# A long-convolution block with an MLP on one Trainium2 core: taps' spectra loaded back in quarters, residuals and joins given to TensorE, and a new order of the operations

## The chip, the cores and the metric

The kernel runs on one core of a Trainium2 chip. Its time is the device time of one execution in microseconds (us); lower is better. A core has a matrix engine (TensorE, PE in the profile), a vector engine (VectorE, DVE), a scalar engine (ScalarE, ACT), a general engine (GpSimd, POOL) and a queue engine (SyncE, SP) that issues most transfers. Each engine works through its own instructions in the order in which they were written and waits for the others through semaphores.

## The reference

All inputs are bfloat16: u is 2048 rows by 512 channels, the state-space part has 128 states for each channel, and the MLP is 512 to 1376 to 512.

```python
def _A_ref(u, A_re, A_im, B_re, B_im, C_re, C_im, log_dt, Dskip):
    ...
    P = jnp.exp(logdA[:, :, None] * l[None, None, :])         # 512 x 128 x 2048, complex
    K = jnp.einsum("dn,dnl,dn->dl", Cc, P, dB).real           # the taps: 512 x 2048
    ...
    Yf = Uf * Kf[None, :, :, :]                               # the spectra of u and of the taps, padded to 4096
    y = irfft2(Yf)[:, :, 0, :L] ...
    return y + u * Dskip[None, None, :]

x = A_u
h = x + _A_ref(_layernorm(x, axis=-1), ...)
h2 = h + (gelu(_layernorm(h) @ w1 + b1) @ w2 + b2)            # tanh form of gelu
```

The layer norm runs over the 512 channels of a row.

## The kernel before, in words

**Tiling.** The 2048 rows are cut into two blocks b = 0 and 1 of 1024, and each block into two halves sb of 512. The 512 channels are cut into four chunks c of 128. The taps are handled for two chunks at a time: q = 0 holds chunks 0 and 1, q = 1 holds chunks 2 and 3. The output of block 1 needs two products of spectra (its own input with the near taps, and block 0's with the far taps), that of block 0 needs one.

**Stages, in the order in which most of the work comes.**

1. Tables: ACT computes exponentials and sines (L1068 is the last kind) from arguments that TensorE writes to PSUM (L1059). DVE multiplies them (L1030, then L1072 for chunks 2 and 3). In the same time the rows of u are normalized: `stats` takes the power on POOL (L926), `unorm` applies it (L947 on DVE or L949 on ACT).
2. Taps: `kgen` (L1101, L1102) makes the taps of chunks 0 and 1 from these products, `kgen4` (L1132, L1133) those of chunks 2 and 3; the result is copied out of PSUM, and a small DVE addition of Dskip (L1115, L1142) ends a chunk.
3. Spectra of the taps, for each q: `carry` issues four small DMAs (L1152) that put a copied strip behind the taps; `kspec` (L1167) transforms in two parts, of which the second needs the carry; `kstage` writes its result to DRAM in two DMAs of 512 KB (the tensor AK_d) and loads it back with another arrangement in two DMAs of 512 KB; `fstage` (L981) works on four of the sixteen f at a time. `lstage` (L1195, L1214) makes the far taps' spectra by way of small DMAs on POOL's queue (AL_d).
4. Spectra of u: `xspec` (L961, L981), block 0 and then block 1.
5. `inverse(b, c, ...)`: for each half fh DVE makes the product (L1243; for block 1 two products and a sum, L1248), for block 1 two more DVE additions join the four parts to two (L1251), and TensorE transforms back: 16 matmuls of 64x128 for two terms, 32 for four (L1259). The result is copied out and transposed by a DMA (L1265).
6. `tail(b, sb)`: TensorE's last step of the transform (L1329); the residual h = u + y, by an identity matmul on TensorE for b = 0, sb = 0 (L1324, then a copy out of PSUM) and by a DVE addition elsewhere (L1336); statistics of the second layer norm (L1339 and small operations); its application (L1352 on DVE or L1354 on ACT); and a transpose.
7. `mlp(b, sb)`: w1 (L1383), gelu on ACT (L1385), w2 (L1405), the residual on DVE (L1407), and the output's DMAs.

**PSUM and copies.** PSUM is used as four slots of 128x1024 float32 (ps_64 to ps_67 in the listings below). Copies out of PSUM have the lines L542 (ACT) and L544 (DVE), whoever asked for them.

**What sets the order.** Each call adds operations to a list. The table ORDER is a permutation of the list's numbers, and the instructions are written in that order; a negative number stands for the second of two engines on which an operation may run. A planner (`Sched.run`) walks through ORDER with costs in us. Its costs don't change the order: they choose which PSUM slot an operation gets, and where the planner sees TensorE idle for over 0.4 us it writes filling matmuls (L1510, an identity matmul of 128x512 whose result nobody reads). Each POOL computation is made to wait for the last DVE instruction written ahead of it.

## Time and profile before

| | before |
|---|---|
| time, median of 3 runs | 236.28 us (236.27 to 236.67) |
| the profiled execution | 235.89 us, of which 234.0 us are the span in the trace |
| TensorE busy | 200.7 us (86%), 2809 matmuls |
| ScalarE busy | 177.3 us (76%) |
| VectorE busy | 170.0 us (73%) |
| GpSimd busy | 39.8 us (17%) |
| mean granted TensorE clock | 0.997 |

The share of an engine is an average over stages with different limits, so it has to be read by stretches of the span. Rows with "x" give a number of instructions; "ar" is SBUF, "ps" is PSUM; the arrow points from the input to the output. "PEld" is TensorE's loading of weights, which runs beside its matmuls. A row of the chain of waits tells what the last-ending work was waiting for at that time: start, duration, engine, output, line. A "[... <-X]" behind a row is the idle time ahead of it and what ended it.

### The profile page before, as it was taken

What the parts mean: (1) busy time and instruction counts of PE and PEld (TensorE: products, weight loads), DVE (VectorE), ACT (ScalarE), POOL (GpSimd) and SP (SyncE); (2) the same over time, 40 slices, a digit from 0 to 9 for tenths busy, and PEclk for the clock granted to TensorE, in tenths of its full rate; (3) what the DMA queues carried; (4) which work ended last, traced back from release to release, by engine and by line L of the source; (5) the groups of instructions that cost most, each with busy time, mean ns of one, the idle gap of its engine ahead of it and who ended that gap; (6) DMA issues with size and microseconds to landing.
All of it is one profiled execution on the core that took longest, in us unless ns stands there. A gap on an engine that the chain in (4) does not pass through costs nothing.

```text
span 234.0 us, 6711 instructions
## 1 busy us (share of the span) xinstructions
PE 200.7 (86%) x2809; PEld 106.9 (46%) x2809; DVE 170.0 (73%) x304; ACT 177.3 (76%) x217; POOL 39.8 (17%) x185
## 2 busy tenths in 40 slices
PE   4206898868888899999989988899999999999993
PEld 2102633325666685456753343344444444444552
DVE  4969989998997764798999889889934884022021
ACT  5999999999999898999989897787275106806600
POOL 7950760000055520040000110100000101000000
PEclk9999999999999999999999999999999999999998
DMA  5692220100000163875589922235632072053103
GB/s 170 165 197 55 59 36 11 37 1 3 3 6 6 30 146 68 244 202 183 112 140 198 311 96 41 49 66 104 114 66 38 0 139 66 0 111 79 34 20 72
DMA packets 39246, 20.33 MB, mean 87 GB/s; under 512 B 26738, under 2 KB 37012, under 8 KB 39216
## 3 DMA queue, kind: packets, MB, share of 16 engines
q1 hardware_dynamic: 38510, 19.28, 36.1%
q0 software_dynamic: 256, 0.30, 0.8%
q8 instruction: 22, 0.36, 0.6%
q10 hardware_dynamic: 450, 0.33, 0.5%
q14 instruction: 8, 0.07, 0.1%
HBM read 8.10 MB, written 4.49 MB: 54 GB/s over the span
## 4 chain that ended last, share of the span: by engine, by line
PE 41%; ACT 13%; DVE 7%; DMA 5%; issue 4%; POOL 3%; SPq 1%; ACTq 0%; DVEq 0%
PE ps L1405 16%; PE ps L1383 13%; ACT ar L542 9%; DMA ar<-ar 3%; PE ps L1329 2%; ACT ar L1068 2%; DMA ar<-AK_d 2%; PE ps L1259 2%; PE ps L981 2%; ACT ar L1385 2%; DVE ar L1248 2%; DVE ar L1243 1%; POOL ar L926 1%; PE ps L961 1%; POOL ar L1466 1%
## 5 line engine op out<-in xcount | busy, mean ns | idle before, releaser
L542 ACT CAST ar<-ps 128x1024 bf16<-128x1024 f32 (+3 forms) x75 | 66.6, 965 | 11.8 <-PE ps L1259 5.1
L1385 ACT ACTIVATE ar<-ps,ar 128x512 bf16<-128x512 f32 (+1 forms) x44 | 28.6, 687 | 25.0 <-PE ps L1383 24.5
L1383 PE MATMUL ps<-ar 128*128 128x512 bf16 (+1 forms) x176 | 40.4, 379 | 1.5 <-ACT ar L542 1.1
L1405 PE MATMUL ps<-ar 128*128 128x512 bf16 (+3 forms) x187 | 39.6, 367 | 0.0
L1068 ACT ACTIVATE ar<-ps 128x1024 bf16<-128x1024 int16 x36 | 34.5, 1058 | 0.5 <-PE ps L1059 0.5
L1407 DVE TENSOR_TENSOR ar<-ps,ar 128x512 bf16<-128x512 f32 (+1 forms) x17 | 10.8, 653 | 29.5 <-PE ps L1405 16.3
L1243 DVE TENSOR_TENSOR ar<-ar 128x2048 bf16<-128x2048 bf16 x24 | 28.8, 1220 | 3.8 <-PE ps L1259 3.0
L1405 PEld LDWEIGHTS <-ar 128*128 128x128 bf16 (+1 forms) x187 | 18.0, 98 | 19.9 <-issue 0.4
L1383 PEld LDWEIGHTS <-ar 128*128 128x128 bf16 (+1 forms) x176 | 17.1, 100 | 21.7 <-issue 3.0
L1059 PE MATMUL ps<-ar 128*32 128x512 f16 (+1 forms) x368 | 21.6, 331 | 5.7 <-ACT ar L1068 5.6
L544 DVE CAST ar<-ps 128x1024 bf16<-128x1024 f32 (+3 forms) x20 | 21.2, 1075 | 7.0 <-PE ps L1133 3.0
L1510 PE MATMUL ps<-ar 128*128 128x512 bf16 x53 | 14.6, 412 | 13.6 <-DMA ar<-in_A_u_dram 12.2
L1030 DVE TENSOR_TENSOR ar<-ar 128x2048 bf16<-128x2048 bf16 x21 | 24.8, 1214 | 0.8 <-ACT ar L1068 0.4
L926 POOL TENSOR_TENSOR ar<-ar 128x4 f32<-128x4 f32 (+1 forms) x6 | 9.3, 1544 | 93.9 <-DVE ar L603 42.2
L801 ACT ACTIVATE ar<-ar 128x1024 bf16<-128x1024 f32 x16 | 15.7, 1041 | 1.1 <-DVE ar L613 1.1
L1059 PEld LDWEIGHTS <-ar 128*32 128x32 f16 x368 | 9.3, 97 | 15.8 <-issue 13.5
L961 PE MATMUL ps<-ar 128*32 128x512 bf16 x256 | 15.9, 380 | 0.2 <-ACT ar L542 0.2
L1259 PE MATMUL ps<-ar 64*128 64x128 bf16 x384 | 13.6, 217 | 1.1 <-ACT ar L542 1.1
L1510 PEld LDWEIGHTS <-ar 128*128 128x128 bf16 x53 | 4.9, 102 | 21.0 <-issue 17.5
L1259 PEld LDWEIGHTS <-ar 64*128 64x128 bf16 x384 | 11.1, 94 | 6.7 <-issue 2.7
L619 DVE SCALAR_TENSOR_TENSOR ar<-ar 128x4 f32<-128x4 f32 (+5 forms) x37 | 10.2, 282 | 5.3 <-POOL ar L926 3.5
L981 PE MATMUL ps<-ar 128*32 128x512 bf16 (+1 forms) x256 | 13.0, 328 | 0.2
(118 smaller groups left out, 293.7 us busy)
## 6 DMA issues: line engine op xcount, KB each, us to landing
ar<-in_A_u_dram SPq DMA_DIRECT2D x4, 512.0 KB
AK_d<-ar SPq DMA_DIRECT2D x4, 512.0 KB
ar<-AK_d SPq DMA_DIRECT2D x4, 512.0 KB
out_dram<-ar SPq DMA_DIRECT2D x30, 64.0 KB
ar<-in_B_w_dram SPq DMA_DIRECT2D x4, 344.0 KB
ar<-ar SPq DMA_DIRECT2D x20, 64.0 KB
ar<-in_B_w_dram SPq DMA_DIRECT2D x2, 640.0 KB
AL_d<-ar POOLq DMA_DIRECT2D x8, 36.0 KB, 4.0
```

The lines of the kernel that those rows point to most:

```text
L542: act.copy(out_fn(), in_fn())
L544: dve.tensor_copy(out_fn(), in_fn())
L961: pe.matmul(pst(p)[32 * cg:32 * cg + 32, 512 * z:512 * z + 512], lhsT=BD.ap()[:, 32 * f + 2 - 2 * jl:32 * f + 34 - 2 * jl], rhs=un[2 * (2 ...
L1030: dve.tensor_tensor(o, o[:, 1].unsqueeze(1).to_broadcast([P] + list(o.shape[1:])), f[:, :, ::-1, ::-1] if rev else f, ALU.mult)
L1059: pe.matmul(pst(p)[32 * g:32 * g + 32, 256 * j:256 * (j + n)].rearrange("p (a b) -> p a b", a=n), lhsT=W2[DELTAS.index(d)].ap(), rhs=S2[g] ...
L1068: add("ACT", c_act(1024), lambda e, o_=o_, i_=i_: act.activation(o_(), i_(), ACT.Sin, scale=SINSC), r=[p, TBL], w=[sc[cs]])
L1243: dve.tensor_tensor(pieces(o).rearrange("p z (a r d) -> p a z r d", a=4, r=2), k, x, ALU.mult)
L1259: pe.matmul(pst(p)[:, 512 * h + 128 * k:512 * h + 128 * k + 128], lhsT=o[z].ap()[rows, k, r, :], rhs=TP[w].ap()[rows, f0 // 2 + k, :], sta ...
L1383: pe.matmul(pst(p)[:fs, 512 * z:512 * z + 512], lhsT=w1s[dc].ap()[:, fc * P:fc * P + fs], rhs=ybuf.ap().rearrange("p (t c) k -> p c t k", ...
L1385: add("ACT", c_act(512, 1), lambda e, p=p, z=z, fc=fc, fs=fs: act.activation(hT.ap()[:fs, fc, :], pst(p)[:fs, 512 * z:512 * z + 512], ACT. ...
L1405: pe.matmul(pst(p)[:, 512 * z + c0:512 * z + c1], lhsT=hT.ap()[:fs, fc, 128 * t:128 * t + 128], rhs=w2s[fc].ap()[:fs, c0:c1], start=(fc == ...
L1510: pe.matmul(slots[z][:, 0:512], lhsT=identb.ap(), rhs=hs[15].ap(), start=True, stop=True)
```

## The change

It has four parts.

- `kstage` loads AK_d back in four DMAs of 256 KB for each q, where there were two of 512 KB; each quarter is one group of `fstage`.
- `tail(0, 1)` puts the residual on TensorE by identity matmuls, as `tail(0, 0)` did: four matmuls of 128x512 more, four DVE additions fewer, and four copies of 128x512 out of PSUM in their place (three on ACT, one on DVE).
- `inverse(1, c)` for c = 0 and 1 leaves out the two DVE joins of each half (8 of 16 in all) and lets TensorE work on four terms: 64 more matmuls of 64x128.
- ORDER is another permutation; the planner's costs for POOL's power (0.3 to 1.5), `kgen4` (0.13 to 0.146) and `tail` (0.85 throughout) are others.

```diff
@@ ORDER
-    49, 1, 0, 50, 2, 12, 15, 5, 52, 11, 13, 40, 3, 16, 88, 74, 17, 167, 4, 51, 43, 18, 19, 73, ...
+    1, 49, 12, 15, 0, 50, 88, 2, 16, 146, 14, 4, 17, 3, 166, 13, 18, 11, 19, 52, 89, 20, 21, 51, ...
@@ stats
-        POOL(0.3, lambda: gp.tensor_tensor(buf[3].ap(), buf[1].ap(), mhalf.ap().to_broadcast([P, n]), ALU.pow), ...
+        POOL(1.5, lambda: gp.tensor_tensor(buf[3].ap(), buf[1].ap(), mhalf.ap().to_broadcast([P, n]), ALU.pow), ...
@@ kgen4
-                add("PE", 0.13 * h, fn, r=[EA2, Br, IA2, Bi], w=[p], new=[p] if b == 0 else [], hv=1)
+                add("PE", 0.146 * h, fn, r=[EA2, Br, IA2, Bi], w=[p], new=[p] if b == 0 else [], hv=1)
@@ kstage
-        for fh in range(2):
-            dma("SP", lambda fh=fh: kf[8 * fh:8 * fh + 8].ap(), lambda fh=fh: D.rearrange("s (q f) d -> (s q) f d", f=16)[:, 8 * fh:8 * fh + 8, :], 524288, [("AK", q, 0), ("AK", q, 1)], [kf[8 * fh:8 * fh + 8], ("KFR", q, fh)], k=0.7)
+        for f0 in range(0, 16, 4):
+            dma("SP", lambda f0=f0: kf[f0:f0 + 4].ap(), lambda f0=f0: D.rearrange("s (q f) d -> (s q) f d", f=16)[:, f0:f0 + 4, :], 262144, [("AK", q, 0), ("AK", q, 1)], [kf[f0:f0 + 4]], k=0.7)
@@ inverse
-            if b:
+            mix = b and c > 1
+            if mix:
                 for r, op in enumerate((ALU.subtract, ALU.add)):
...
-            terms = [(0, 0, 0), (0, 1, 2)] if b else [(0, 0, 0), (1, 1, 1), (0, 1, 2), (1, 0, 2)]
+            terms = [(0, 0, 0), (0, 1, 2)] if mix else [(0, 0, 0), (1, 1, 1), (0, 1, 2), (1, 0, 2)]
...
-            add("PE", 0.235 * len(terms), fn, r=(o[:1] if b else o) + TP, w=[p], new=[p])
+            add("PE", 0.235 * len(terms), fn, r=(o[:1] if mix else o) + TP, w=[p], new=[p])
@@ tail
-                    if first:
+                    if b == 0:
                         pe.matmul(o, lhsT=identb.ap(), rhs=hs[8 * b + j].ap(), start=True, stop=False)
...
-            add("PE", 0.85 if first else 0.43 * (1 + b), fn, ...
+            add("PE", 0.85, fn, ...
...
-                if not first:
+                if b:
                     add("DVE", c_dve(512, 1, True), lambda e, src=src, hh=hh: dve.tensor_tensor(hh.ap(), src(), hh.ap(), ALU.add), ...
```

Over the whole program this makes 960 operations of 964, and 47 filling matmuls of 53 (from the spectra on 17 of 22). Of the copies out of PSUM and the second layer norm, some change engine: four copies of `kspec` go from ACT to DVE, four of 128x4x256 from DVE to ACT, and four applications L1354 from ACT to DVE as L1352. One line is added ahead of `inverse`'s end, so lines from L1249 on are one higher after the change (L1251 becomes L1252, L1329 becomes L1330).

**VectorE where the taps of chunks 0 and 1 end.** The rows are VectorE's, before, from the first product of chunks 2 and 3 that stands ahead of chunk 0's addition; `128x33x10` is a copy of taps of chunk 1, the small L619 and L603 belong to the layer norm of u, and the L619 behind L1115 uses the power that POOL computes.

```order
L1072 TENSOR_TENSOR ar<-ar 128x16x128 x2
L1115 TENSOR_TENSOR ar<-ar 128x32
L619 SCALAR_TENSOR_TENSOR ar<-ar 128x8
L1072 TENSOR_TENSOR ar<-ar 128x16x128
L947 TENSOR_SCALAR ar<-ar 128x512
L603 TENSOR_TENSOR ar<-ar 128x8
L1072 TENSOR_TENSOR ar<-ar 128x16x128
L544 CAST ar<-ps_67 128x33x10
L1115 TENSOR_TENSOR ar<-ar 128x32
```

The same place after the change:

```order
L1072 TENSOR_TENSOR ar<-ar 128x16x128
L1115 TENSOR_TENSOR ar<-ar 128x32
L934 BN_STATS ar<-ar 128x6
L544 CAST ar<-ps_64 128x33x10
L1115 TENSOR_TENSOR ar<-ar 128x32
L1072 TENSOR_TENSOR ar<-ar 128x16x128
L619 SCALAR_TENSOR_TENSOR ar<-ar 128x8
L1072 TENSOR_TENSOR ar<-ar 128x16x128 x2
L619 SCALAR_TENSOR_TENSOR ar<-ar 128x8
```

The second L1115, which completes the taps of q = 0, stood behind four products L1072 and behind the L619 that waits for POOL; now it stands behind one product and ahead of that L619. On TensorE the two parts of `kspec` for q = 0, with `lstage`'s L1195 between them, now follow one another ahead of all of `kgen4`; before, 48 matmuls of `kgen4` stood ahead of the second part. They stand behind the last L1059, as before. The four matmuls L1451 (a selection of table rows that L1214 needs), which stood between the last L1059 and `kspec`, now stand amid block 0's inverse.

**SP's queue of transfers around the spectra.** Before, from the carry of q = 0 on (`ar<-ar 7x...` is a carry, AK_d_68 is q = 0, AK_d_69 is q = 1, in_B_w_dram are weights of the MLP):

```order
L1152 DMA ar<-ar 7x2048 x4
L554 DMA AK_d_68<-ar 128x8x256 x2
L1152 DMA ar<-ar 7x32x64 x4
L554 DMA ar<-AK_d_68 128x2048 x2
L554 DMA AK_d_69<-ar 128x8x256 x2
L554 DMA ar<-in_B_w_dram 96x512
L554 DMA ar<-AL_d_70 18x4x256 x4
L554 DMA ar<-AK_d_69 128x2048 x2
```

And after:

```order
L1152 DMA ar<-ar 7x2048 x4
L554 DMA AK_d_68<-ar 128x8x256 x2
L554 DMA ar<-AK_d_68 128x1024 x3
L554 DMA ar<-in_B_w_dram 128x5x512
L1152 DMA ar<-ar 7x32x64 x3
L554 DMA ar<-in_B_w_dram 128x1376
L1152 DMA ar<-ar 7x32x64
L554 DMA ar<-AK_d_68 128x1024
L554 DMA ar<-in_B_w_dram 128x1376
L554 DMA ar<-AL_d_70 18x4x256
L554 DMA AK_d_69<-ar 128x8x256 x2
```

Three quarters of q = 0 now stand ahead of the carry of q = 1, and weights of 640 KB (128x5x512) and twice 344 KB (128x1376) stand between the quarters, the carry and the rest; before, these weights came after the first transposes.

**VectorE in the stretch where block 0's tail meets block 1's inverse.** Before, from the pair of products behind the statistics of block 0's first half:

```order
L1243 TENSOR_TENSOR ar<-ar 128x4x2x256 x2
L1352 TENSOR_SCALAR ar<-ar 128x512
L1248 TENSOR_TENSOR ar<-ar 128x2048
L1336 TENSOR_TENSOR ar<-ps_64,ar 128x512
L1251 TENSOR_TENSOR ar<-ar 128x4x128
L1339 BN_STATS ar<-ar 128x6
L1251 TENSOR_TENSOR ar<-ar 128x4x128
L1336 TENSOR_TENSOR ar<-ps_64,ar 128x512
L1339 BN_STATS ar<-ar 128x6
L1243 TENSOR_TENSOR ar<-ar 128x4x2x256
```

And after:

```order
L1243 TENSOR_TENSOR ar<-ar 128x4x2x256
L1340 BN_STATS ar<-ar 128x6
L619 SCALAR_TENSOR_TENSOR ar<-ar 128x4
L1353 TENSOR_SCALAR ar<-ar 128x512 x3
L1243 TENSOR_TENSOR ar<-ar 128x4x2x256
L1340 BN_STATS ar<-ar 128x6
L1248 TENSOR_TENSOR ar<-ar 128x2048
L1340 BN_STATS ar<-ar 128x6
L1243 TENSOR_TENSOR ar<-ar 128x4x2x256 x2
L1340 BN_STATS ar<-ar 128x6
```

The residual additions (L1336) and the joins (L1251) are gone from here; three applications of the second layer norm (L1353) stand together where one stood.

6 lines of the change are left out of this document (3 added, 3 removed), and 66 rows, old and new, of the table ORDER.

## The prediction

> **What bounds the kernel now.** I read the busy time of each engine by stretches first, then the chain of waits, then single groups. Columns of the stretches: length, TensorE (PE) with its matmuls, weight loads, DVE, ACT, POOL, granted clock, DMA share, GB/s.
>
> ```profile
> 5.00:77.00 72.00, 50.22 (x1135) 29.12 (x1139) 66.25 (x134) 71.15 (x84) 24.95 (x112) 1.00 0.23 50
> 70.00:77.00 7.00, 5.50 (x219) 4.11 (x211) 5.42 (x12) 7.00 (x10) 3.29 (x1) 1.00 0.02 5
> 77.00:98.40 21.40, 21.33 (x360) 13.76 (x360) 14.40 (x28) 19.13 (x24) 4.23 (x5) 1.00 0.47 116
> 98.40:118.00 19.60, 19.21 (x496) 12.79 (x497) 17.45 (x17) 18.55 (x21) 2.40 (x4) 1.00 0.69 178
> 118.00:136.00 18.00, 16.98 (x246) 7.72 (x246) 15.35 (x24) 16.70 (x20) 1.55 (x2) 1.00 0.90 225
> 136.00:154.00 18.00, 15.27 (x145) 7.22 (x144) 16.36 (x26) 15.41 (x22) 1.06 (x1) 1.00 0.17 34
> 154.00:224.00 70.00, 69.84 (x392) 32.26 (x391) 35.52 (x65) 33.81 (x50) 2.02 (x2) 1.00 0.35 68
> ```
>
> Until 77 us the tables bound it: ACT is busy for 71.15 of 72 us. From 77 on TensorE does. Its idle time is 0.07 + 0.39 up to 118, 1.02 + 2.73 from 118 to 154, and 0.16 behind: 4.2 us up to 154, of which 3.75 lie in the two stretches from 118. In those DVE is busy for 15.35 and 16.36 of 18, and the chain runs over it:
>
> ```profile
> 134.99 0.57 PE ps L1259 x16
> 135.59 2.36 DVE ar L1243 x2
> ...
> 145.41 1.01 ACT ar L542
> ```
>
> So three things change the end: when TensorE's closed stretch starts (about 77), what work it holds, and the holes from 118 to 154.
>
> **The change part by part.** The sum is made on the profiled execution: span 234.0, time 235.89, so 1.89 around it. The median 236.28 is 0.39 above, which I add at the end.
>
> *Start of the closed stretch.* The rows at its edge:
>
> ```profile
> 74.47 2.00 ACT L1068 ACTIVATE ar<-ps 128x1024 bf16<-128x1024 int16 x2
> 76.29 0.88 ACT L949 ACTIVATE ar<-ar 128x512 bf16<-128x512 bf16 x1
> 74.55 0.64 PE L1059 MATMUL ps<-ar 128*32 128x256 f16 x16
> 75.00 0.40 PE L1451 MATMUL ps<-ar 128*32 128x512 bf16 x4
> 76.92 1.04 PE L1167 MATMUL ps<-ar 20*128 20x512 bf16 x16 [0.94 <-DVE ar L1115]
> 71.65 0.20 DVE L1115 TENSOR_TENSOR ar<-ar 128x32 bf16<-128x32 bf16 x1
> 73.32 0.17 DVE L619 SCALAR_TENSOR_TENSOR ar<-ar 128x8 f32<-128x8 f32 x1 [1.48 <-POOL ar L926]
> 76.69 0.18 DVE L1115 TENSOR_TENSOR ar<-ar 128x32 bf16<-128x32 bf16 x1
> 77.61 1.16 DVE L1072 TENSOR_TENSOR ar<-ar 128x2048 bf16<-128x2048 bf16 x1
> ```
>
> The first part of `kspec` waits for the L1115 at 76.69, which stands in DVE's queue behind the 1.48 us wait for POOL and several products. With L1115 ahead of those, what holds `kspec` is the last L1059 group in front of it. That needs a slot which the third last sine frees: the sines end at 74.47 + 2.00 = 76.47, two sines of 1.0 earlier is 74.47, and with 0.64 of matmuls it is 75.1. So the stretch starts 76.92 − 75.1 = **1.8 us** earlier. The bounds are 0.8 (the last L1059 held by one sine more) and 2.4 (it ends at 74.55, when it began here). The four L1451 leave this gap and come back inside the closed stretch: **+0.4**.
>
> The second part of `kspec` now follows without the `kgen4` that covered the carry. SP's queue prices that:
>
> ```profile
> 76.92 3.04 SPq L1152 DMA_DIRECT2D ar<-ar  x4
> 82.28 1.04 PE L1167 MATMUL ps<-ar 27*128 27x512 bf16 x16
> ```
>
> Issuing the carry takes 3.04 us from the last L1115 on. Landing took at most 82.28 − 79.96 = 2.3 us more, since nothing waited for it. That L1115 comes at about 72 in the new order: the 71.65 at which the first one starts here, less one product of 1.16, plus a copy and a BN_STATS of about 1.1 and the table work before. The carry is then down by 72 + 5.3 = 77.3. The second part is due at 75.1 + 1.04 + 1.1 (L1195, the same size by columns) = 77.2. I take nothing; at worst 0.3 us, and the copies of `kgen4` that wait in turn would be late by as much.
>
> *Work added to TensorE.* A set of 16 matmuls L1259 costs 0.57 us (chain row above) and one of 32 costs 1.08; the residual is read from the tail of block 0, both forms of which the chain shows:
>
> ```profile
> 120.46 1.08 PE ps L1259 x32
> 127.80 0.55 PE ps L1329 x4
> 128.35 0.32 PE ps L1324
> 128.68 0.34 PE ps L1329 x2
> 132.83 1.62 PE ps L1510 x7
> ```
>
> Joins: four groups of 16 become 32, 4 × (1.08 − 0.57) = +2.04. Residual: a quarter of a tail costs 0.55 / 2 = 0.275 without the identity matmul and 0.32 + 0.34 = 0.66 with it, 4 × 0.385 = +1.54. Together **+3.6 us**. All of it lies in the closed stretch or in front of it, so it counts whole unless it falls into a hole.
>
> *Filling matmuls.* From the spectra on there are 17 instead of 22, at 1.62 / 7 = 0.23 us each: 5 × 0.23 = **−1.2**. A filling matmul costs time only where work stood ready behind it; at worst they go and leave idle time, 0.
>
> *The holes.* The groups in 118 to 154, by form (busy us, mean ns):
>
> ```profile
> L1251 DVE TENSOR_TENSOR ar<-ar 128x512 bf16<-128x512 bf16 x8 | 3.3, 419 | 0.0
> L1336 DVE TENSOR_TENSOR ar<-ps,ar 128x512 bf16<-128x512 f32 x4 | 2.6, 682 | 0.0
> L542 ACT CAST ar<-ps 128x512 bf16<-128x512 f32 x4 | 2.1, 588 | 0.6 <-PE ps L1329 0.6
> L1510 PE MATMUL ps<-ar 128*128 128x512 bf16 x22 | 5.4, 380 | 0.9 <-ACT ar L542 0.9
> L1354 ACT ACTIVATE ar<-ar 128x512 bf16<-128x512 bf16 x3 | 2.2, 806 | 0.0
> L1352 DVE TENSOR_SCALAR ar<-ar 128x512 bf16<-128x512 bf16 x1 | 0.4, 409 | 0.0
> ```
>
> DVE loses 3.3 (joins) and 2.6 (additions) and gains one copy of about 0.65 and two or three L1352 (0.4 each, 1.0): −4.3 of its 31.7 us here. ACT gains three copies, 3 × 0.59 = 1.8, and loses two or three L1354 at 0.81, about 2: no change. The idle 3.75 us and the 5.4 us of filling both come from waits for DVE's products and for what DVE hands to ACT. DVE's queue gets 4.3 us shorter, and the matmuls added (3.6) want room just there. I let TensorE's 4.2 us of idle time shrink by **−3.0**. The bounds: 0, if ACT, unchanged and at 32.1 of 36 us, sets the pace instead; −4.2, if every hole closes. I am nearer to the second because the relief of DVE is larger than all the holes, and DVE, not ACT, carries most pieces of the chain from 135.59 to 145.4.
>
> *The quarters.* In the chain the load of AK_d ends at 93.38 + 4.98 = 98.4, but next to nothing stood idle for it:
>
> ```profile
> 93.38 4.98 DMA ar<-AK_d
> 93.38 1.01 SPq L554 DMA_DIRECT2D ar<-AK_d  x2
> 89.91 3.35 SPq L1152 DMA_DIRECT2D ar<-ar  x4
> ```
>
> The work in between is `xspec`'s, which is ready beforehand; the stretch 77 to 98.4 has 0.07 us idle. Issuing two loads takes 1.01 us of SP's time, so two more cost SP 1.0 per q, hidden as long as the `xspec` work lasts. They now stand ahead of the carry of q = 1, and so are issued earlier than at 93.38. I take 0. The bounds: −0.13 (a third of the 0.39 idle in the next stretch) and +3 (rivals 2 and 5).
>
> **The sum.** −1.8 + 0.4 + 3.6 − 1.2 − 3.0 = −2.0. The profiled execution would come to 233.9, and with 0.39 the forecast is **234.3 us**.
>
> **The rivals.**
>
> 1. *ACT takes DVE's place, slower.* The place is 118 to 154, where ACT is busy for 32.1 of 36 us and is handed three copies. If the holes stay because copies out of PSUM arrive no earlier, the added 3.6 count whole: −1.8 + 0.4 + 3.6 − 1.2 = +1.0, **237.3 us**. It decides once less than 1 us of idle time is taken up. For it: the largest releasers of the groups there are copies L542 (0.9 before L1510). Against it: the chain from 135.59 to 145.4 is DVE but for single pieces. Chance 0.20.
> 2. *Weights ahead of the carry, no change.* In the new queue 640 KB and 344 KB of weights stand ahead of the last carry of q = 1 and of the fourth quarter. At the 317 GB/s that the best stretch shows, they take 3.1 us:
>
> ```profile
> 130.00:136.00 6.00, 6.00 (x71) 2.45 (x72) 4.37 (x13) 5.56 (x8) 1.55 (x2) 1.00 0.98 317
> ```
>
>    A carry that lands that late holds the second part of `kspec` for q = 1 and with it half of the spectra. About 1 us lies under `xspec`, so TensorE stands for 2 us: 234.3 + 2 = **236.3 us**. Against it: the DMA share from 77 to 98.4 is 0.47. Chance 0.11.
> 3. *The holes close and more.* All 4.2 go, and the other filling matmuls yield to work: −2.0 − 1.2 = −3.2, **233.1 us**; and where the time in which the other 17 filling matmuls ran (17 × 0.23 = 3.9) is used by a third as well, **231.8 us**. For it: DVE's relief exceeds the holes. Chance 0.12.
> 4. *The lead is lost again at `kgen4`, a gain of half a microsecond or none.* TensorE would start 1.8 us earlier but waits for ACT's copies of 0.87 us each and the 1.28 us table load:
>
> ```profile
> 80.83 0.88 ACT L542 CAST ar<-ps 128x792 bf16<-128x792 f32 x1 [0.16 <-PE ps L1133]
> 81.73 1.28 ACT L536 ACT_TABLE_LOAD   x1
> ```
>
>    Then 1.4 of the 1.8 are gone: **235.7 us**. Against it: ACT also begins its copies of `kspec` at 76.5 instead of 78.0, with an L949 less. Chance 0.12.
> 5. *The quarters land one after the other, slower.* A small carry lands within 2.3 us of its issue; were that a fixed share which each quarter pays in turn, four would take 9.2 us where two halves took 4.98, 4.2 later. For q = 0 the 3.35 us of carry that no longer stand ahead cover most, for q = 1 the inverse of chunks 0 and 1 covers half: 0.9 + 2.1 = +3.0, **237.3 us**. Against it: the two halves, 1 MB, came in 4.98 us together. Chance 0.03.
>
> The Trainium skill has such a rule ("SBUF — State Buffer", section "The DMA setup-cost knee"): each transfer pays some 2 us that don't grow with its bytes, so transfers should be joined, not split. By its formula two quarters more per q would cost, as an estimate, about 4 us if none of that overlapped, which is rival 5; the two halves of 512 KB above took less than the 6.4 us that it gives for two in turn, so the trace bears out little of it.
>
> That the change doesn't do what it says is no rival: the listings show each edit in place.
>
> **How the numbers follow.** The forecast's own case has 0.42. A measurement here can tell about 0.2%, 0.5 us, from no change. Faster (under 235.8): the forecast 0.42, rival 3's 0.12 and 0.08 of rival 4, together 0.62. Same (235.8 to 236.75): 0.08 of rival 2 and 0.04 of rival 4, 0.12. Slower: rival 1's 0.20, rival 5's 0.03 and 0.03 of rival 2, 0.26. The forecast's own range is 233.1 to 235.4 (the holes from −4.2 to −1.9). The whole range has to hold 8 in 10 and reaches to rivals 1 and 3: **231.9 to 237.4**.
>
> **What would show it.** Start: the first L1167 at about 75.1 without a wait for L1115, and no wait of the second part for the carry over 0.4. Work: 448 matmuls L1259, eight L1325, 47 of L1511. Holes: PE's idle time in the 36 us before the main run of L1383 down from 3.75 to about 1, with DVE's busy time there down by about 4. Quarters: no L981 waiting for AK_d. Right for the wrong reason it would be if the time fell and those holes stayed. Wrong it would be if ACT L542 ended waits of L1260 and L1384 for over 3 us in that stretch (rival 1), or if L1168 waited for L1152 (rival 2).

## The result and the profile after

The changed kernel takes 239.59 us at the median of four runs (237.8 to 242.05) where the kernel before takes 236.28. The ratio is 1.0117, with a 95% interval of 1.0074 to 1.016. The forecast was 234.3 us with a range of 231.9 to 237.4, and faster was thought the likeliest. The change makes the kernel **slower**, and the forecast was wrong in sign and in size.

The execution profiled first (242.05 us, span 240.1) was a disturbed one, and the ratios here and below leave such runs out, so they are not quotients of the medians. The main readings are taken from a second profiled execution of the same kernel (the first experiment below): 237.81 us, span 235.9, against 234.0 before. All line numbers of the changed kernel from L1249 on are one higher than before.

The stretches of that second profile, with the columns of the forecast's first table, and then one line for all of it from the first `kspec` matmul to the end:

```profile
77.00:98.40 21.40, 20.53 (x360) 13.96 (x360) 15.76 (x34) 18.65 (x22) 4.45 (x5) 1.00 0.63 171
98.40:118.00 19.60, 19.48 (x468) 11.49 (x458) 17.83 (x19) 18.45 (x21) 2.40 (x4) 1.00 0.77 175
118.00:136.00 18.00, 17.04 (x292) 8.55 (x287) 14.13 (x19) 15.76 (x19) 0.98 (x1) 1.00 0.80 166
136.00:154.00 18.00, 16.23 (x203) 8.60 (x203) 14.43 (x22) 15.92 (x22) 1.58 (x3) 1.00 0.16 31
76.98:235.90 158.92, 150.81 (x1740) 78.83 (x1736) 102.49 (x163) 103.14 (x130) 11.43 (x14) 1.00 0.46 100
```

And the same line of the kernel before, from its first `kspec` matmul:

```profile
76.92:234.00 157.08, 148.73 (x1669) 77.05 (x1669) 101.89 (x163) 103.69 (x132) 11.26 (x14) 1.00 0.45 102
```

These two last lines hold the account of this execution. TensorE's closed stretch starts at 76.98 instead of 76.92 (+0.06). It holds 150.81 us of work instead of 148.73 (+2.1). Its idle time is 158.92 − 150.81 = 8.11 instead of 8.35 (−0.24). Together +1.9 us, which is the difference of the spans. The work came as the forecast said; the earlier start and the closed holes, −1.8 and −3.0 in the forecast, did not. A third profile of the same kernel (under "The change, the weights, and the copies on one chip") divides its loss otherwise:

```profile
76.56:236.40 159.84, 150.06 (x1729) 78.69 (x1736) 102.69 (x163) 103.10 (x130) 11.43 (x14) 1.00 0.46 100
```

There the start is 0.36 us earlier than before, and the idle time is 9.78 us, 1.4 more than before. (It has 11 matmul records fewer than the second profile, so some of this idle time may be work.) Single terms hold to a microsecond or so, not to a tenth. What all three profiles share is that most of the forecast's gains are missing.

**The edge at 77 us**, in the changed kernel:

```profile
72.66 0.76 ACT L542 CAST ar<-ps 128x726 bf16<-128x726 f32 x1 [0.70 <-PE ps L1102]
73.33 5.04 ACT L1068 ACTIVATE ar<-ps 128x1024 bf16<-128x1024 int16 x5
74.04 0.50 DVE L544 CAST ar<-ps 128x330 bf16<-128x330 f32 x1 [1.59 <-PE ps L1102]
74.65 0.17 DVE L1115 TENSOR_TENSOR ar<-ar 128x32 bf16<-128x32 bf16 x1
75.71 1.34 PE L1059 MATMUL ps<-ar 128*32 128x256 f16 x32
76.98 1.04 PE L1167 MATMUL ps<-ar 20*128 20x512 bf16 x16
79.04 1.55 PE L1167 MATMUL ps<-ar 27*128 27x512 bf16 x16
```

The last L1115 comes at 74.65 instead of 76.69, and the first L1167 no longer waits for it. But the sines now end at 73.33 + 5.04 = 78.37 instead of 76.47, so the last two L1059 groups run from 75.71 to 77.05, and L1167 stands behind them on TensorE. VectorE's copy ahead of the L1115 now waits 1.59 us for TensorE's `kgen`.

**TensorE's waits** from 77 us on (total, times, longest), of the kernel before; the wait of 0.9 for L1115, shown in the forecast, is left out:

```profile
PE ps L1383 <- ACT ar L542: 1.1, 2, 0.6
PE ps L1259 <- ACT ar L542: 1.1, 2, 0.9
PE ps L1510 <- ACT ar L542: 0.9, 1, 0.9
PE ps L1214 <- ACT ar L542: 0.5, 1, 0.5
PE ps L961 <- ACT ar L542: 0.2, 1, 0.2
PE ps L1383 <- ACT ar L1385: 0.2, 1, 0.2
```

And of the changed kernel:

```profile
PE ps L1214 <- ACT ar L542: 1.1, 1, 1.1
PE ps L981 <- DMA ar<-AK_d: 0.7, 2, 0.4
PE ps L1330 <- DMA ar<-ar: 0.7, 1, 0.7
PE ps L1384 <- DMA ar<-ar: 0.7, 1, 0.7
PE ps L1363 <- ACT ar L1355: 0.4, 1, 0.4
PE ps L1511 <- ACT ar L542: 0.3, 1, 0.3
PE ps L1260 <- ACT ar L1386: 0.2, 1, 0.2
```

Waits that ACT ends fell from 4.0 to 2.0. Waits that transfers end rose from nothing to 2.1: 0.7 for the quarters of AK_d (before 98.4 us), and 0.7 + 0.7 for the transposes ahead of a tail (L1330, between 118 and 136) and of an MLP matmul (L1384, behind 154). In total the waits moved from one releaser to another.

**The work**, by groups of equal shape from L1167 on. Before (matmuls, us busy, mean ns):

```profile
L1259 PE MATMUL ps<-ar 64*128 64x128 bf16 x384 | 13.6, 217 | 1.1 <-ACT ar L542 1.1
L1329 PE MATMUL ps<-ar 128*64 128x512 bf16 x48 | 6.7, 387 | 0.0
L1324 PE MATMUL ps<-ar 128*128 128x512 bf16 x4 | 1.6, 390 | 0.0
```

After:

```profile
L1260 PE MATMUL ps<-ar 64*128 64x128 bf16 x448 | 15.0, 217 | 0.2 <-ACT ar L1386 0.2
L1330 PE MATMUL ps<-ar 128*64 128x512 bf16 x48 | 7.1, 388 | 0.7 <-DMA ar<-ar 0.7
L1325 PE MATMUL ps<-ar 128*128 128x512 bf16 x8 | 3.1, 387 | 0.0
L1511 PE MATMUL ps<-ar 128*128 128x512 bf16 x17 | 4.4, 381 | 0.3 <-ACT ar L542 0.3
```

Joins +1.4, residual +1.5 and +0.4, filling matmuls 5.4 to 4.4, −1.0. The moved L1451 and the gap of the carry (below) add to this.

### The profile page after: what moved, and what is told of

It is laid out like the page before. It is cut to its first block, busy times and chain, and to the rows that moved or that the text cites. A ratio compares the mean times of both kernels' runs of the same rounds, so it can differ in the third digit from the quotient of the medians.

```text
span 240.1 us, 6815 instructions
## 1 busy us (share of the span) xinstructions
PE 205.4 (86%) x2855; PEld 109.4 (46%) x2871; DVE 171.6 (71%) x303; ACT 175.6 (73%) x213; POOL 37.4 (16%) x182
## 4 chain that ended last, share of the span: by engine, by line
PE 49%; ACT 23%; DMA 13%; DVE 5%; issue 5%; SPq 3%; POOL 1%; ACTq 0%; DVEq 0%; POOLq 0%
PE ps L1384 15%; PE ps L1406 13%; ACT ar L1068 9%; DMA ar<-ar 7%; DMA ar<-AK_d 4%; ACT ar L801 4%; PE ps L1260 3%; PE ps L961 3%; PE ps L1330 3%; ACT ar L626 3%; SPq L554 2%; PE ps L981 2%; ACT ar L1007 2%; ACT ar L1004 2%; ACT ar L542 2%
## 5 line engine op out<-in xcount | busy, mean ns | idle before, releaser
L542 ACT CAST ar<-ps 128x1024 bf16<-128x1024 f32 (+4 forms) x77 | 68.3, 948 | 13.7 <-PE ps L1260 4.9
L1384 PE MATMUL ps<-ar 128*128 128x512 bf16 (+1 forms) x176 | 42.5, 390 | 0.7 <-DMA ar<-ar 0.7
L544 DVE CAST ar<-ps 128x1024 bf16<-128x1024 f32 (+5 forms) x22 | 22.7, 1039 | 10.4 <-PE ps L981 4.6
L1384 PEld LDWEIGHTS <-ar 128*128 128x128 bf16 (+1 forms) x176 | 17.5, 102 | 22.7 <-issue 4.0
L1059 PE MATMUL ps<-ar 128*32 128x512 f16 (+1 forms) x368 | 22.9, 343 | 5.2 <-ACT ar L1068 4.9
L926 POOL TENSOR_TENSOR ar<-ar 128x4 f32<-128x4 f32 (+1 forms) x6 | 7.5, 1252 | 95.8 <-DVE ar L603 76.7
L981 PE MATMUL ps<-ar 128*32 128x256 bf16 (+1 forms) x256 | 13.7, 328 | 3.4 <-DMA ar<-AK_d 3.1
L1059 PEld LDWEIGHTS <-ar 128*32 128x32 f16 x368 | 9.1, 98 | 15.8 <-issue 13.8
L1260 PE MATMUL ps<-ar 64*128 64x128 bf16 x448 | 15.0, 217 | 0.2 <-ACT ar L1386 0.2
L1260 PEld LDWEIGHTS <-ar 64*128 64x128 bf16 x448 | 12.7, 94 | 5.0 <-issue 2.9
L1511 PE MATMUL ps<-ar 128*128 128x512 bf16 x39 | 12.9, 439 | 1.3 <-issue 0.5
L603 DVE TENSOR_TENSOR ar<-ar 128x1 f32<-128x1 f32 (+9 forms) x35 | 10.6, 308 | 3.5 <-POOL ar L682 2.1
L619 DVE SCALAR_TENSOR_TENSOR ar<-ar 128x4 f32<-128x4 f32 (+5 forms) x37 | 10.1, 283 | 4.0 <-POOL ar L926 2.3
```

The source lines that it names most:

```text
L542: act.copy(out_fn(), in_fn())
L544: dve.tensor_copy(out_fn(), in_fn())
L1059: pe.matmul(pst(p)[32 * g:32 * g + 32, 256 * j:256 * (j + n)].rearrange("p (a b) -> p a b", a=n), lhsT=W2[DELTAS.index(d)].ap(), rhs=S2[g] ...
L1260: pe.matmul(pst(p)[:, 512 * h + 128 * k:512 * h + 128 * k + 128], lhsT=o[z].ap()[rows, k, r, :], rhs=TP[w].ap()[rows, f0 // 2 + k, :], sta ...
L1384: pe.matmul(pst(p)[:fs, 512 * z:512 * z + 512], lhsT=w1s[dc].ap()[:, fc * P:fc * P + fs], rhs=ybuf.ap().rearrange("p (t c) k -> p c t k", ...
```

## The experiments

The theory before them: the added work on TensorE is real, and nothing pays for it, since the start is held by the sines and AK_d's weights stand ahead in SP's queue. The rival: ScalarE sets the pace where the residual's copies were handed to it. Kernels sent together ran on one chip and share its runs of the kernel before; there are five such groups. Every ratio is to the kernel before on the same chip, with its 95% interval.

### The change once more

No edit.

> The changed kernel itself, for a second profile. Theory O (the new order: it takes away the work that covered the carry, the loads of AK_d and the transposes, and lets TensorE's granted clock fall to a half for 3.4 us where it runs thin): 238 to 241 us, spread over more than 1 us from run to run, with a stretch of clock 0.5 and about 4 us of TensorE idle time between 75 and 118 us in the trace. Theory W (the added 3.6 us of TensorE work is simply not paid back): 238 to 240, but without a wait for AK_d or the carry of more than 0.5 us.

Measured: 239.25 us, ratio 1.0094 (1.0056 to 1.0131). The slowdown repeats in another group of runs. Its profile is the one read above. Neither theory fits whole: between 75 and 118 us the granted clock is full and the idle time from 77 on is 1.0 us, not 4, but TensorE does wait 0.7 us for AK_d.

### The edits in the order of before

The three edits in the code, with before's order and costs (its numbers shifted to the new list of operations).

```diff
 ORDER = [ ...
-  rows of the change
+  rows of the kernel before, with the joins and additions of the edits dropped
```

> The three edits (quarters, residual and joins on TensorE) in the kernel before, with its order and its planner's costs. Theory O: the edits by themselves cost little, 235.0 to 237.0. Theory W: the added work counts whole, 238.5 to 240.

Measured: 238.42 us, 1.0096 (1.0064 to 1.0127). So a loss of this size comes without the new order too (the new order has 1.0047 to 1.0117 over three groups of runs). The two largest waits of TensorE in this kernel, from 77 us on:

```profile
PE ps L1260 <- ACT ar L542: 2.0, 4, 0.8
PE ps L1384 <- ACT ar L542: 0.9, 2, 0.5
```

Here copies on ACT end 2.0 + 0.9 us of waits of the inverse and the MLP: rival 1's place. But the next kernel, which leaves the residual's copies out and loses nothing, has 1.8 + 1.0 us at the same two lines, so these waits alone don't price the residual.

### The joins alone, in the order of before

```diff
-            if b:
+            mix = b and c > 1
+            if mix:
...
-            terms = [(0, 0, 0), (0, 1, 2)] if b else [...]
+            terms = [(0, 0, 0), (0, 1, 2)] if mix else [...]
```

> Only the joins of chunks 0 and 1 of block 1 on TensorE, in the order before (64 more matmuls, 8 DVE operations fewer, 2.0 us of TensorE work). Theory O: 235.5 to 236.8, since DVE's 3.3 us less fill holes. Theory W: 238.0 to 238.6.

Measured: 236.61 us, 1.0013 (0.9993 to 1.0034), no difference that can be measured. The group of the joins in this kernel:

```profile
L1260 PE MATMUL ps<-ar 64*128 64x128 bf16 x448 | 15.5, 217 | 1.8 <-ACT ar L542 1.8
```

It takes 15.5 us against 13.6 before, +1.9 (the forecast said 2.04), and the 16 filling matmuls left take 4.0 against 5.4, −1.4. So the joins are nearly paid for by filling matmuls that were not needed any more.

### The residual alone, in the order of before

```diff
-                    if first:
+                    if b == 0:
                         pe.matmul(o, lhsT=identb.ap(), rhs=hs[8 * b + j].ap(), ...)
...
-                if not first:
+                if b:
                     add("DVE", ..., dve.tensor_tensor(hh, src, hh, ALU.add) ...)
                 else:
                     evac(...)
```

> Only the residual of block 0's second half on TensorE, in the order before (1.5 us more of TensorE work, four DVE additions replaced by copies). Theory O: 235.5 to 236.8. Theory W: 237.5 to 238.2.

Measured: 237.75 us, 1.007 (1.0045 to 1.0095). Of the two edits that were tried alone, this one costs. The quarters alone were not tried in this order; the joins' 0.0013 and the residual's 0.0070 leave 0.0013 of the 0.0096 to them and to what the edits do together.

### The weights behind the transposes

In the changed kernel, three loads of weights leave their place on SP's queue. The rows of SP, L554 being loads and stores and L1152 the carry:

```diff
 L554 DMA ar<-AK_d 128x1024 x3
-L554 DMA ar<-in_B_w_dram 128x5x512
-L1152 DMA ar<-ar 7x32x64 x3
-L554 DMA ar<-in_B_w_dram 128x1376
-L1152 DMA ar<-ar 7x32x64
+L1152 DMA ar<-ar 7x32x64 x4
 L554 DMA ar<-AK_d 128x1024
-L554 DMA ar<-in_B_w_dram 128x1376
...
 L1266 DMA_TRANSPOSE ar<-ar 128x16x128 x4
+L554 DMA ar<-in_B_w_dram 128x5x512
+L554 DMA ar<-in_B_w_dram 128x1376 x2
```

> The changed kernel with three loads of MLP weights (640 KB and twice 344 KB) moved in SP's queue from between the carry of q = 1 and the loads of AK_d to behind the first four transposes, where most weights stood before. Theory D (the new queue makes AK_d's loads late; that is the part of the loss that differs from run to run): TensorE waits for AK_d fall under 0.3 us in all, the median falls by 1 to 2 us to 237.3 to 238.3, and the runs lie closer together. Theory E (the quarters themselves or the clock make the spread): no change, 238.8 to 239.8, spread as before.

Measured: 236.91 us, 1.0004 (0.9981 to 1.0026), in a group of runs where the kernel before takes 236.79. That is below even the range of theory D. No wait for AK_d is left. From this group alone it looked as if the weights were the whole loss; the fourth group of runs, below, corrects that.

### The early part as before

The first 320 operations (up to about 67 us) in before's order, the rest as changed.

> The changed kernel, with the first 320 operations (to about 67 us) in the order of the kernel before and the rest in the changed order. Theory T (the new order's tables end 1.9 us later, and that ate the earlier start): the last sine ends at about 77 instead of 78.4, the first L1167 starts at 75.5 to 76.2 instead of 77.0, and the median falls by about 1 us to 238.0 to 238.6. If the lead of the start is lost later in any case, the first L1167 starts as early, but the median stays at 239.0 to 239.6.

Measured: 237.53 us, 1.0035 (1.0013 to 1.0056). The start is not won: the last sine ends at 78.12 and L1167 starts at 76.88. ACT's sines now wait for their inputs:

```profile
71.12 1.04 ACT L1068 ACTIVATE ar<-ps 128x1024 bf16<-128x1024 int16 x1 [0.76 <-PE ps L1059]
75.26 2.86 ACT L1068 ACTIVATE ar<-ps 128x1024 bf16<-128x1024 int16 x3 [0.55 <-PE ps L1059]
```

In the changed kernel 0.6 of the sines' 1.9 us is there before that: ACT's operation L626 of 128x2048 starts at 68.86 instead of 68.26. Here it starts at 68.27, so the early part accounts for this 0.6 us, and the rest arises beside the sines from there on. AK_d again ends 2.7 us of waits here.

### The early start alone

The kernel before, with only the last L1115 and its copy moved ahead of the last two products of this stretch on VectorE:

```diff
 L603 TENSOR_TENSOR ar<-ar 128x8
-L1072 TENSOR_TENSOR ar<-ar 128x16x128
 L544 CAST ar<-ps 128x33x10
 L1115 TENSOR_TENSOR ar<-ar 128x32
+L1072 TENSOR_TENSOR ar<-ar 128x16x128
+L1072 TENSOR_TENSOR ar<-ar 128x16x128
...
-L1072 TENSOR_TENSOR ar<-ar 128x16x128
 L544 CAST ar<-ps 128x132x6
```

> The kernel before, and only VectorE's order where the taps of chunk 1 end changed: the copy 128x33x10 and its L1115 stand ahead of the third last product L1072, and the last product directly behind that one. No edit else. If an earlier start of kspec is worth its full time: first L1167 at 75.5 to 75.8 instead of 76.9, kgen4 at 78.0 instead of 79.0, 235.0 to 235.4 us. If the lead is lost further on (ACT's copies, the transfers): 235.9 to 236.3.

Measured: 236.51 us, 0.9986 (0.9961 to 1.0012), no difference. Lines of this kernel are one higher again (L1168 is before's L1167, L1116 its L1115):

```profile
75.62 0.50 DVE L545 CAST ar<-ps 128x330 bf16<-128x330 f32 x1 [0.60 <-PE ps L1103]
76.47 1.04 PE L1168 MATMUL ps<-ar 20*128 20x512 bf16 x16 [0.22 <-DVE ar L1116]
78.53 1.04 PE L1511 MATMUL ps<-ar 128*128 128x512 bf16 x3
```

L1168 starts 0.45 us earlier than L1167 did, not 1.8, since VectorE's copy now waits 0.60 for TensorE's matmuls (L1103). And the next piece, `kgen4`, comes at 79.40 where it came at 78.98. It isn't VectorE's products that hold it: the last of them ends at 78.67 here and ended at 78.77 before. The three filling matmuls above, which the planner wrote into a gap that it expected, keep TensorE until 79.57, and the chain of waits runs over them to `kgen4` with no other engine in between. From L1168 on, filling matmuls take 6.3 us here and 5.4 before. What this kernel takes without the three was not tried.

### The new order without the edits

The changed order and costs, all three edits undone:

```diff
-            mix = b and c > 1
+            mix = bool(b)
...
-                    if b == 0:
+                    if first:
...
-                if b:
+                if not first:
...
-        for f0 in range(0, 16, 4):   # four loads of 256 KB
+        for fh in range(2):          # two loads of 512 KB
```

> The new order with all three edits undone (halves, residual and joins on VectorE, each join right behind its sum). If the edits are what costs and the order is neutral: 236 to 237. If the order costs by itself: 237.5 to 239.5, with the tables ending 1.9 us later and waits for AK_d as in the changed kernel.

Measured: 243.15 us, 1.029 (1.0244 to 1.0336), far slower than either kernel and outside both expectations. TensorE waits 2.3 us at L1214 for a copy on ACT and 0.9 at L1384 for a residual addition, and from L1167 on it runs 11.7 us of filling matmuls (39 of them) where the changed kernel runs 4.4 (17). The new order was made for the edits; what it is worth can't be read without them, nor the edits' worth by undoing one of them in it. The next three runs have to be read with that in mind.

### Residual, joins and quarters undone one at a time

Three kernels, each the one with the weights behind the transposes and one edit undone in the changed order: the residual (`if b == 0` to `if first`, `if b` to `if not first`), the joins (`mix = bool(b)`), and the quarters (halves again).

> The changed kernel with the weights later (as the run before), and the residual of block 0's second half back on VectorE. Theory R (the residual's 1.5 us of TensorE work is never paid back, as alone in the old order): 1.0 to 1.6 us below the kernel with the weights later, ratio to before 0.993 to 0.997. Theory P (this order leaves VectorE no room for the four additions): ratio 1.000 to 1.008.

> The changed kernel with the weights later, and the joins of chunks 0 and 1 of block 1 back on VectorE, each right behind its sum. If VectorE's relief pays for the 64 matmuls: 0 to 2 us above the kernel with the weights later, ratio 1.000 to 1.009. If the matmuls count whole: 2 us below it, ratio 0.992.

> The changed kernel with the weights later, and AK_d loaded back in halves, each in the place of the earlier of its two quarters. If quarters are worth nothing: within 0.3 us of the kernel with the weights later, ratio 0.999 to 1.002. If quarters start the work on a group earlier: TensorE waits for AK_d again, 0.5 to 1.5 us more.

Measured: 239.25 us, 1.0098 (1.0063 to 1.0134) without the residual; 238.64, 1.0076 (1.0048 to 1.0105) without the joins; 238.75, 1.0091 (1.0063 to 1.0118) with halves. The kernel that they are to be compared with, with all edits and the weights behind the transposes, did not run in this group; it has 1.0004 and 1.0021 in two others. The kernel of the next section ran in this group and in the fourth, with 1.0056 and 1.0038, so ratios may lie some 0.2% higher here. Even so, undoing any edit gains nothing. Without the residual, TensorE waits 2.1 us at L1214 instead of 1.1; without the joins, 1.3 there and 0.5 at L982 (the L981 of the other listings) for copies on ACT. Filling matmuls take 7.1 and 8.8 us from L1167 on, against 4.0 in both profiles of the kernel with all edits, so more of TensorE's waiting is hidden in its busy time than these waits show. The first lies just above the range of theory P, the second in the range for VectorE's relief. Both agree with the reading that this order counts on VectorE's room, but neither shows it.

For the halves the trace shows where the time goes. TensorE's rows around the first group of AK_d with halves, and the same group with quarters (the second profile of that kernel); in both the `xspec` matmuls in front start at 88.49:

```profile
90.76 1.04 PE L1511 MATMUL ps<-ar 128*128 128x512 bf16 x3
92.02 1.06 PE L981 MATMUL ps<-ar 128*32 128x256 bf16 x32 [0.22 <-DMA ar<-AK_d]
```

```profile
90.87 1.28 PE L981 MATMUL ps<-ar 128*32 128x256 bf16 x32
```

With halves the group starts 1.15 us later, behind three filling matmuls that hide most of the wait. At `lstage`'s L1195, a few pieces on, the difference is 0.93 us (99.94 against 99.01), and the spans differ by 0.8 (235.4 and 234.6). So in this order the quarters do start a group earlier, as the second theory said, and are worth about 0.9 us in these two profiles; the wait that it named is not seen because it was filled.

### One sine and one L1059 group earlier

The kernel with the weights behind the transposes, with ACT's copy of 128x726 (it waited 0.70 us for L1102 in the changed kernel's second profile) one sine later, and one L1059 group on TensorE ahead of the last `kgen` part:

```diff
 L1068 ACTIVATE ar<-ps 128x4x8x32
-L542 CAST ar<-ps 128x2x33x11
 L1068 ACTIVATE ar<-ps 128x4x8x32
+L542 CAST ar<-ps 128x2x33x11
```

> The changed kernel with the weights later, and two things moved at the end of the tables: ACT's copy of the taps 128x726 of chunk 1 one sine later (with the copy and L1115 behind it), and one group L1059 ahead of the last part of kgen. Theory T (the sines' wait of 0.7 us for kgen holds the start): the last sine ends 0.4 to 0.7 us earlier, L1167 starts as much earlier, ratio 0.997 to 0.999. If the start isn't what counts: 1.000 to 1.002.

> The changed kernel with the weights later, one copy of taps later and one group L1059 earlier at the end of the tables, beside the kernel with the weights later alone. Theory T (the sines' wait for kgen holds the start): last sine 0.4 to 0.7 us earlier, L1167 as much, ratio 0.3 percent below the kernel with the weights later. If the start isn't what counts: the same ratio within 0.1 percent.

Measured: 238.03 us, 1.0056 (1.0028 to 1.0084) with the three above, and 237.64, 1.0038 (1.0008 to 1.0067) with the next three. The profile of the second:

```profile
76.38 1.94 ACT L1068 ACTIVATE ar<-ps 128x1024 bf16<-128x1024 int16 x2 [0.62 <-DVE ar L619]
```

The sines end at 78.32 and L1167 starts at 76.64. The copy no longer stands in their way, but now the last pair waits for VectorE. The kernel without this step has L1167 at 76.68 and 76.33 in its two profiles, with waits of the copy of only 0.19 and 0.27 us, so there was less to win than the 0.70 promised. This, the early part as before, and the early start alone are three ways to buy back the start; none made the kernel faster.

### The change, the weights, and the copies on one chip

Two repeats without an edit, so that both meet the same chip:

> The changed kernel once more, as the base of the next two on one chip: 238.5 to 239.6 us, ratio to before 1.008 to 1.013, single runs spread over 3 us or more.

> The changed kernel with the three weight loads behind the first transposes, beside the changed kernel on the same chip. Theory D (weights ahead of the carry and of AK_d's last quarters are worth 1 to 2 us): ratio to before 0.999 to 1.004, and at least 1 us below the changed kernel. If the earlier low value came from the chip that it ran on: ratio 1.006 to 1.011, less than 0.7 us below.

Measured: 237.99 us, 1.0047 (1.0013 to 1.008) for the change, lower than expected; 237.36, 1.0021 (0.999 to 1.0052) with the weights behind the transposes. In the change's profile here TensorE waits 2.3 us for AK_d, and in that of the first execution 3.1, more than the 0.7 in the profile read above. With the weights behind the transposes this wait is gone, as in the other profile of that kernel. So the wait for AK_d in the changed kernel is caused by the weights ahead of it; the times put 0.6 us on it, but the two intervals overlap, and this amount isn't settled.

The third kernel of this group takes the residual alone in before's order and gives four of its copies to VectorE, in the places where the additions had stood. ACT loses:

```diff
-L542 CAST ar<-ps 128x512 x2
...
-L542 CAST ar<-ps 128x512
...
-L542 CAST ar<-ps 128x512
```

VectorE gains four `L544 CAST ar<-ps 128x512`.

> The residual on TensorE in the old order, as alone before, but its four copies out of PSUM on VectorE instead of ScalarE. If ScalarE's 2.4 us of copies are what makes the edit cost 1.6 us (ScalarE takes VectorE's place): ratio 1.000 to 1.003. If TensorE's 1.5 us simply count: 1.005 to 1.008, as with the copies on ScalarE.

Measured: 236.44 us, 0.999 (0.9964 to 1.0015), against 1.007 with the copies on ACT (on another chip). The identity matmuls are in this kernel as in that one, so it looks as if it were the copies on ACT that cost, in that order. But the two kernels ran in different groups, and the changed kernel's own ratio moved by as much (0.7%) between groups; the two were not run side by side.

### The copies on VectorE, in both orders

In the changed order (with the weights behind the transposes) four copies of 128x512 behind the tails were moved from ACT to VectorE, and in before's order with all three edits likewise. In both listings:

```diff
-L542 CAST ar<-ps 128x512 x4      (ACT, in several places)
+L544 CAST ar<-ps 128x512 x2      (DVE)
+L544 CAST ar<-ps 128x512 x2      (DVE, two places)
```

The first expectation counts three copies on ScalarE, as the sum of both halves' tails has it; in this order all four of the second half stood there, and all four were moved.

> The changed kernel with the weights later and the residual's three copies on ScalarE moved to VectorE (all four there). Theory S (ScalarE's copies are what the residual costs): ratio to before 0.995 to 0.999, some 0.3 to 0.7 percent under the kernel with the weights later (1.0004 and 1.0021). If ScalarE has room in this order: 1.001 to 1.006.

> The three edits in the order before, with the residual's four copies on VectorE. Theory S: ratio 1.000 to 1.004, against 1.0096 with the copies on ScalarE. If TensorE's added 3.6 us count by themselves: 1.007 to 1.011.

Measured: 240.4 us, 1.0164 (1.0127 to 1.0202) in the changed order; 237.87, 1.0049 (1.0025 to 1.0073) in the old one, against 1.0096 with the copies on ACT. By these ratios the same move helps one order by about half a per cent, with intervals that overlap a little and from two groups, and harms the other by 1.4. The first is outside both expectations, the second between them.

In the old order VectorE's statistics (L1340) wait 4.3 us for copies on ACT when the residual's copies are there, and 0.6 when they are on VectorE. TensorE's largest wait hardly changes; it was 2.0 with the copies on ACT:

```profile
PE ps L1260 <- ACT ar L542: 1.9, 3, 1.0
```

In the changed order the loss begins at the second layer norm: two of the copies stand on VectorE ahead of its small operations, of which L619 comes at 134.77 instead of 133.20, and TensorE runs 14 filling matmuls there instead of 6. Later TensorE waits 2.3 us at L1214 for a copy on ACT, where it waited 1.1. That this second wait is the same lateness passed on is argued, not followed through the trace.

## Why the prediction was wrong, step by step

**The start, −1.8: wrong, measured +0.06.** The sentence that failed is "what holds `kspec` is the last L1059 group in front of it", with the sines taken to end where they ended before. The L1115 did come 2 us earlier. But the matmuls of `kgen` that feed it were pulled ahead of L1059 on TensorE, and its last copy ahead of three sines on ACT; this copy of 128x726 waits 0.70 us there with five sines behind it, where two stood. The sines end 1.9 us later, about what the earlier L1115 had gained: 0.6 of it is there at 68.9 us already, 0.7 is that wait, and the rest was not followed. I priced the moved step on VectorE's queue alone and not on the queues of TensorE and ACT, which produce its input. The size is not fixed: the three profiles of the changed kernel have L1167 at 77.08, 76.98 and 76.56, and the two with the weights behind the transposes, whose order is the same up to there, at 76.68 and 76.33. So between nothing and 0.6 us of the 1.8 was won; the forecast's lower bound was 0.8.

**The carry, at most 0.3: mis-sized.** It rested on "that L1115 comes at about 72"; it came at 74.65. In the chain the carry's landing stands right ahead of the second part of `kspec`:

```profile
77.23 2.29 DMA ar<-ar
79.56 1.04 PE ps L1167 x15
```

It ends at 79.52, so the second part's first matmul, at 79.04, was followed by a gap: 1.55 us instead of 1.04, 0.5 more. The row counts this gap as busy time.

**Added work less filling, +0.4 + 3.6 − 1.2 = +2.8: about right, measured +2.1.** By groups the joins and the residual came to 1.4 + 1.5 + 0.4 = 3.3, and the filling matmuls to −1.0.

**The holes, −3.0: wrong, measured −0.24** over the whole stretch from L1167 on. Between 118 and 154 us the idle time is 0.96 + 1.77 = 2.73, where it was 3.75. DVE's busy time there fell by 31.71 − 28.56 = 3.2 instead of 4.3, ACT's by 0.4 ("no change" holds in the new order). The waits that ACT ends fell from 4.0 to 2.0 us, all of them in this stretch. The sentence "I am nearer to the second because the relief of DVE is larger than all the holes" counted one releaser only. With DVE relieved, ACT still ends 2.0 us of waits there, 1.1 of them at L1214 where it was 0.5, and a transfer now ends 0.7 (L1330). Outside the stretch transfers end 1.4 us more that were not there before, and before 98.4 the idle time rose from 0.07 to 0.87. Rival 3, all holes closed, is ruled out by the same rows.

**The quarters, 0: part of it wrong, and rival 2 half right.** What arrived late was AK_d itself: 0.7 to 3.1 us of waits in the three profiles of the changed kernel. Rival 2 had the right queue, weights ahead on SP's, but let them hold the carry. No wait for the carry of q = 1 was seen. With these weights behind the transposes the wait is gone. SP's queue around it shows why (start, us for the row, which is SP's time and not the transfer's):

```profile
87.64 1.29 SPq L554 DMA_DIRECT2D ar<-AK_d  x3
89.04 0.39 SPq L554 DMA_DIRECT2D ar<-in_B_w_dram  x1
90.36 2.55 SPq L1152 DMA_DIRECT2D ar<-ar  x3
92.96 0.93 SPq L554 DMA_DIRECT2D ar<-in_B_w_dram  x1
93.93 0.81 SPq L1152 DMA_DIRECT2D ar<-ar  x1
94.78 0.86 SPq L554 DMA_DIRECT2D ar<-AK_d  x1
```

The fourth quarter is issued 6 us after the third, behind two loads of weights and the carry. Rival 5, a fixed price per quarter paid in turn, is not borne out: with the weights behind the transposes TensorE waits for no quarter, and with halves in that order the first group starts 1.15 us later.

**Rival 1, ACT takes DVE's place, at 0.20: likely in the old order, not shown.** There the ratios are lower with the residual's copies off ACT (1.007 and 0.999; 1.0096 and 1.0049 with all the edits), but each pair comes from two groups of runs, and TensorE's waits for ACT's copies do not fall with them. Its number, 237.3 us, which is rival 5's too, is the nearest of all cases to what was measured, because it is the sum without the holes; that is luck, since in the changed order ACT was not busier than before, and it is the start that is missing as well. The sign that the forecast named for it, over 3 us of waits of L1260 and L1384 for ACT's copies, is absent there, and the copies cost more on VectorE than on ACT.

**Rival 4, the lead lost at `kgen4`**, had no lead to lose in the changed kernel. In the early start alone the lead was lost at that very place, but not to ACT's copies or the table load: `kgen4` was 0.42 later although L1168 was 0.45 earlier, behind three filling matmuls.

What stays open: the ratio of the same changed kernel was 1.0117, 1.0094 and 1.0047 in three groups of runs, which no profile explains; how much of the loss is the wait for AK_d; and how much of the filling matmuls' time, which differs from kernel to kernel, stood in front of work that was ready. No kernel tried here beats the kernel before by more than the measurement can tell (0.9986 and 0.999 are the best).

## What to carry to other kernels

When a step is moved ahead, price it on the queue of every engine that produces its input, not on the one from which it is freed: here an L1115 that came 2 us earlier made the sines end 1.9 us later. Before a hole is counted as closed, ask which releaser comes second, and count bulk loads at their place in the queue that issues them. Count filling matmuls together with idle time, because they hide waits: the cost of halves was found only there. Which engine copies a result out of PSUM may decide whether an edit costs anything, and an order fitted to a set of edits can't be used to price these edits one by one.

## What the runs showed of the hardware

**Half clock after a thin stretch.** In the first profiled execution of the changed kernel, two neighbouring stretches of 3.40 us:

```profile
149.40:152.80 3.40, 2.04 (x50) 1.50 (x50) 1.91 (x6) 3.17 (x5) 0.00 (x0) 0.99 0.68 125
152.80:156.20 3.40, 3.40 (x12) 1.17 (x10) 2.12 (x3) 2.30 (x3) 0.61 (x1) 0.50 0.02 5
```

After a stretch in which TensorE was busy for 2.04 of 3.40 us with 50 small matmuls, the granted clock was 0.50 for one stretch. The second profile, without such a stretch behind 77 us, is slower than before all the same, so this dip isn't the cause. It has half clock earlier, at about 25 to 28 and 38 to 42 us, where the kernel before has none before its end. That such dips in the tables cost little is suggested by the two profiles with the weights behind the transposes: one has a clock of about 0.50 from 24 to 30 us, the other shows full clock until its end, and the spans are 234.7 and 234.6. The Trainium skill ("TensorE: Matmul & The Clock Gate", section "Part 1: The HAM clock gate (the "warmup" mystery)") says that the clock is either full or half, set by windows of about 3.4 us; the 0.50 and the 3.4 us agree with it. Another trace does not: in the profile of the first run with one sine and one L1059 group earlier (300.46 us) the granted clock is 0.65 from 30 us to the end, in every stretch, so half is not the only value below full.

**An operation on VectorE held up beside GpSimd.** A VectorE operation L613 in the tables of the changed kernel, a memset of GpSimd beside it, and the same L613 before:

```profile
17.06 2.20 DVE L613 TENSOR_SCALAR ar<-ar 128x512 f16<-128x512 f32 x1
16.32 2.66 POOL L1417 MEMSET ar<- 128x3072 bf16 x1 [3.10 <-DVE ar L619]
```

```profile
17.33 0.43 DVE L613 TENSOR_SCALAR ar<-ar 128x512 f16<-128x512 f32 x1
```

It lasted 2.20 us instead of 0.43, up to 19.26, just after the memset ended (18.98). All three profiles of the changed kernel show the 2.20 us. The Trainium skill ("SBUF — State Buffer", section "Who interferes with whom") states that a tensor_scalar can take the port pair that VectorE shares with GpSimd and that one then blocks the other for the whole instruction; these rows agree. That it was the memset, and not something else in those 2.66 us, was not tried alone.
